# Softmax steps over the whole batch in even pairs, and a prologue in another order, in a fused softmax convolution and cosine feed-forward kernel

## The chip, the cores and the metric

The kernel runs on one core of one Trainium2 chip. Five engines run side by side, each through its own instructions in the order in which they were written: TensorE (PE, with its weight loads PEld), VectorE (DVE), ScalarE (ACT), GpSimd (POOL) and SyncE (SP), which issues the DMAs. The metric is device microseconds (us) of one execution.

## The reference

```python
w = weight_gen - np.max(weight_gen, axis=-1, keepdims=True)   # (8, 4096, 8 heads, 7 taps)
w = np.exp(w)
w = w / (np.sum(w, axis=-1, keepdims=True) + 1e-09)
x_pad = np.concatenate([np.zeros((B, K - 1, D)), x], axis=1)  # x (8, 4096, 192)
out = np.einsum('bshk,bskhg->bshg', w, x_unf)                 # x_unf: the 7 rows that end at s
...
h = x @ w_in        # x is that out, 32768 x 192; w_in 192 x 2048
g = h * np.cos(h)
return g @ w_out    # 2048 x 192
```

A causal convolution of seven taps, whose weights are a softmax per token and head, feeds a feed-forward layer with the activation h cos h. Inputs and output are float32; the two weight matrices arrive as 64-bit words.

## The kernel before

**Tiles.** The 32768 tokens are laid out as 128 partitions of 256 rows. A *block* is four rows of every partition (512 tokens); there are 64. The 2048 hidden columns are eight *pairs* of 128-column chunks, so the main loop (L678) runs over 64 x 8 = 512 pairs `i`, and eight pairs behind it (`j = i - LAG`) runs the second product. Each product is kept near float32 by splitting operands into a rounded `hi` and a bfloat16 `lo` rest.

**One pair of the loop** is a chain over three engines. PE makes `h` (1024 columns, PSUM, three buffers) from the block's `x_hi`, `x_lo`, `x_b` (`ffn_in_first` L428, `ffn_in_second` L445). ACT rounds it (`turn`, L455), DVE takes the fraction (L459), ACT the sine with a shift, the cosine (L463), DVE the product (L466), ACT the `ghi` part (L473) and DVE the rest `glo` (L477), after which the buffer of `h` is free. Eight pairs later PE multiplies `ghi` and `glo` by `w_out` (`ffn_out`, L519). Every second `ffn_out` carries transposes of one row of a later block (L407). With `k` the place of an `ffn_out` in its four, `evacuate` gives ACT the copies of the transposed row when k is 1 (L535, L536) and of the whole accumulator `part` when k is 3 (L541), both in odd pairs; the pair behind it gets ACT's `x_hi` and POOL's `x_b` and `x_lo` of that row (`split`, L385 to L390).

**POOL** mixes the blocks: `attention` (L331) is seven products of rows and tap weights (L344) and six adds (L359) per block, two steps per pair (three in some early pairs), one block after another; a block's transposes on PE need its last add, and `until_mixed` puts what is missing of a block into the program before PE's first transpose of it, at the pair with `i % 8 == 6`.

**The softmax** of 16 rows (four blocks) is one generator, `softmax` (L263), of which one step runs in each pair, behind that pair's other work; a batch starts at pairs 9, 41, 73, ... Its steps: load, maximum on DVE (L276), subtraction and clamp on POOL (L278, L285), then `powers` (L196) for the exponential without ACT's exponential table, on two halves of 448 columns in turn: nearest multiple (ACT, L206), rest (POOL, L209, L211), two squares (ACT, L214), their product (POOL, L217 to L221), the power of two (ACT, L224), one more square (ACT, L228) and the product (POOL, L231). Then the sum of the taps (POOL, `add_taps`, L187, and L297), the reciprocal (DVE, L303) and the scaling (POOL, L309). Batches with `early` set, the first three, use ACT's exponential (L282) before the sine table is loaded.

**Before the loop** the first block is mixed by `mix_first` (L634): DVE makes seven products, and PE transposes and adds each in PSUM (L631). Weights are converted from 64-bit words by `two_parts` (L128): ACT makes the size (L139), DVE three steps on the bits (L141, L145, L149), ACT the `hi` (L152) and POOL the `lo` (L155); the finished word stands in a tile `t` of which there are three. The table `late` (L590) tells at which pair the later weights are converted. PE's first pairs wait for these.

The program is written in the order in which every engine runs it (L755 to L763 pin that order), so the code sets what stands ahead of what in each queue.

Of the kernel before, what the change touches and what calls it, by code (L numbers as in the profile page):

```python
# [50 lines left out]
def tile_softmax_conv_then_cos_ffn(  # L51
# [76 lines left out]
    def two_parts(raw, hi, lo, half=None):  # L128
# [23 lines left out]
        nc.scalar.copy(out=hi, in_=bits.bitcast(F32))  # L152
# [2 lines left out]
        nc.gpsimd.tensor_tensor(out=lo, in0=bits.bitcast(F32), in1=hi.bitcast(F32), op=ALU.subtract)  # L155
# [40 lines left out]
    def powers(t):  # L196

        (a1, b1), (a2, b2) = EXP_A
        n = t.shape[1]
# [8 lines left out]
        def rest(k):
            nc.gpsimd.tensor_scalar(  # L209
                out=side[k], in0=whole[k], scalar1=-LN_2, scalar2=1.0, op0=ALU.mult, op1=ALU.mult)  # L210
            nc.gpsimd.tensor_tensor(out=t[k], in0=side[k], in1=t[k], op=ALU.add)  # L211

        def square(k, to, a):
            nc.scalar.activation(out=to[k], in_=t[k], func=AF.Square, bias=a, scale=0.5)  # L214

        def quartic(k):
            nc.gpsimd.tensor_scalar(  # L217
                out=side[k], in0=side[k], scalar1=b1, scalar2=1.0, op0=ALU.add, op1=ALU.mult)
            nc.gpsimd.tensor_scalar(
                out=t[k], in0=t[k], scalar1=b2, scalar2=1.0, op0=ALU.add, op1=ALU.mult)  # L220
            nc.gpsimd.tensor_tensor(out=t[k], in0=t[k], in1=side[k], op=ALU.mult)  # L221

        def power(k):
            nc.scalar.activation(  # L224
                out=whole[k], in_=whole[k], func=AF.Relu, bias=ONE_BITS, scale=2.0 ** 23)
# [568 lines left out]
```

## Time and profile before

| | |
|---|---|
| three runs, median (lowest to highest) | 2228.36 us (2226.72 to 2228.66) |
| the profiled execution | 2226.02 us |
| its span, first to last instruction | 2224.2 us |
| PE busy | 2160.8 us, 97% of the span |
| POOL busy | 2015.8 us, 91% |
| DVE, ACT busy | 1900.0 us (85%), 1869.2 us (84%) |
| mean granted clock of TensorE | 0.989 of full speed |

"Busy" leaves out waits; matmuls overlap, so a busy PE is not a PE at its peak. In a timeline row stand the start and the length in us, the engine, the source line, the operation, the tile written and the tiles read, their shapes and the count; the bracket gives the idle time of the engine before it and what ended it. The chain of work that ended last runs for 55% of the span on PE and for 40% on POOL. The granted clock is full from 90 us on; before, it changes between half and full. In 40 equal slices PE is busy in 5 to 7 tenths of the first two, and in 9 or more of all the others but the last.

### The profile page before, as it was taken

The numbers are of one execution on the slowest core, as the hardware profiler recorded it, in microseconds if no ns is written. First come the engines' busy times: TensorE is split into PE (matmuls) and PEld (weight loads), VectorE is DVE, ScalarE is ACT, GpSimd is POOL, SyncE is SP. The second block draws the span as 40 slices with busy tenths as digits, with TensorE's granted clock in tenths as the row PEclk, the third lists the DMA queues.
The fourth block names the chain that finished last, engine by engine and source line by source line (L and its number), as shares of the span: only waits on it lengthen the run. The fifth ranks groups of instructions, "written<-read, shape, count | busy, mean of one in ns | idle before, by whom it ended". The sixth has DMA issues, their size and how long they took to land.

```text
span 2224.2 us, 62220 instructions
## 1 busy us (share of the span) xinstructions
PE 2160.8 (97%) x26552; PEld 1677.8 (75%) x26552; DVE 1900.0 (85%) x1638; ACT 1869.2 (84%) x2352; POOL 2015.8 (91%) x1778
## 2 busy tenths in 40 slices
PE   5699999999999999999999999999999999999998
PEld 3477777777777777777777777777777777777777
DVE  6888888888888888888888888888888888888886
ACT  4688888988888898888988888888888988888885
POOL 8999999999999999999999999999999999989830
PEclk7899999999999999999999999999999999999999
DMA  7221221221221221211211221211212112212100
GB/s 176 49 48 34 56 48 38 51 48 39 51 56 30 59 48 30 60 43 43 52 42 45 48 50 39 56 42 40 56 34 56 48 34 56 48 36 48 30 16 19
DMA packets 53285, 105.67 MB, mean 48 GB/s; under 512 B 5791, under 2 KB 42135, under 8 KB 53007
## 3 DMA queue, kind: packets, MB, share of 16 engines
q1 hardware_dynamic: 53006, 101.69, 19.2%
q8 instruction: 208, 3.41, 0.7%
q14 instruction: 71, 0.57, 0.1%
HBM read 76.50 MB, written 25.17 MB: 46 GB/s over the span
## 4 chain that ended last, share of the span: by engine, by line
PE 55%; POOL 40%; issue 2%; ACT 1%; DVE 1%; DMA 0%; POOLq 0%; SPq 0%; ACTq 0%; DVEq 0%
PE acc L519 27%; PE h L445 17%; POOL xa L359 14%; POOL pr L344 11%; PE h L428 9%; POOL x_lo L390 3%; POOL part L550 2%; POOL taps L211 1%; POOL taps L221 1%; POOL taps L231 1%; POOL x_b L387 1%; POOL xa L344 1%; POOL den L193 1%; PE acc L407 1%; POOL side L209 1%
## 5 line engine op out<-in xcount | busy, mean ns | idle before, releaser
L459 DVE TENSOR_TENSOR turn<-h,turn 128x1024 f32<-128x1024 f32 x512 | 625.7, 1222 | 275.8 <-ACT turn L455 275.2
L519 PE MATMUL acc<-wo,ghi 64*128 64x384 f32 x8096 | 805.9, 336 | 1.8 <-DVE t L149 1.5
L519 PEld LDWEIGHTS acc<-wo,ghi 64*128 64x128 f32 x8096 | 724.5, 184 | 55.2 <-ACT part L541 10.8
L463 ACT ACTIVATE turn<-turn 128x1024 f32<-128x1024 f32 x512 | 541.7, 1058 | 216.3 <-DVE turn L459 216.3
L359 POOL TENSOR_TENSOR xa<-xa,pr 128x768 f32<-128x768 f32 (+1 forms) x384 | 698.6, 1819 | 1.7
L466 DVE SCALAR_TENSOR_TENSOR h<-h,turn 128x1024 f32<-128x1024 f32 x512 | 630.8, 1232 | 2.5 <-ACT turn L463 2.5
L477 DVE TENSOR_TENSOR glo<-h,ghi 128x1024 bf16<-128x1024 f32 x512 | 621.3, 1214 | 1.1 <-ACT ghi L473 1.1
L455 ACT ACTIVATE turn<-h 128x1024 int32<-128x1024 f32 x512 | 523.6, 1023 | 84.9 <-PE h L445 76.2
L344 POOL TENSOR_TENSOR pr<-xt,taps 128x768 f32<-128x768 f32 (+1 forms) x384 | 588.2, 1532 | 5.2
L473 ACT CAST ghi<-h 128x1024 fp32r<-128x1024 f32 x512 | 516.6, 1009 | 2.9 <-DVE h L466 1.3
L519 PE MATMUL acc<-wo_b,glo 64*128 64x192 bf16 x8096 | 462.5, 243 | 0.1
L519 PEld LDWEIGHTS <-glo 64*128 64x128 bf16 (+1 forms) x8128 | 318.1, 94 | 85.8 <-issue 67.7
L428 PE MATMUL h<-x_hi,wa_hi 64*128 64x512 f32 x1024 | 300.8, 583 | 0.0
L445 PE MATMUL h<-x_hi,wa_hi 64*128 64x512 f32 x1024 | 299.9, 582 | 0.0
L428 PE MATMUL h<-x_lo,wa_hi 64*128 64x512 bf16 x1024 | 199.0, 384 | 31.6 <-DVE glo L477 23.5
L445 PE MATMUL h<-x_hi,wb_hi 64*128 64x512 f32 x1024 | 204.2, 395 | 0.0
L428 PE MATMUL h<-x_b,wa_lo 64*128 64x512 bf16 x1024 | 196.7, 380 | 3.5 <-POOL wa_lo L155 3.5
L445 PE MATMUL h<-x_lo,wa_hi 64*128 64x512 bf16 x1024 | 196.0, 379 | 0.8
L445 PE MATMUL h<-x_b,wa_lo 64*128 64x512 bf16 x1024 | 196.2, 379 | 0.0
L445 PE MATMUL h<-x_lo,wb_hi 64*128 64x512 bf16 x1024 | 195.8, 379 | 0.0
L445 PE MATMUL h<-x_b,wb_lo 64*128 64x512 bf16 x1024 | 195.8, 378 | 0.0
L387 POOL TENSOR_SCALAR x_b<-x_hi 128x256 bf16<-128x256 f32 (+1 forms) x247 | 103.6, 420 | 93.0 <-ACT x_hi L385 90.6
(87 smaller groups left out, 2000.3 us busy)
## 6 DMA issues: line engine op xcount, KB each, us to landing
xt<-in_x_dram SPq DMA_DIRECT2D x62, 960.0 KB, 7.0
out_dram<-part SPq DMA_DIRECT2D x256, 96.0 KB, 2.2
taps<-in_weight_gen_dram SPq DMA_DIRECT2D x15, 448.0 KB, 4.5
raw<-in_moe_w_out_dram SPq DMA_DIRECT2D x8, 384.0 KB, 12.2
raw<-in_moe_w_in_dram SPq DMA_DIRECT2D x10, 256.0 KB, 11.1
xt<-in_x_dram SPq DMA_DIRECT2D x1, 768.0 KB, 10.0
xt<-in_x_dram SPq DMA_DIRECT2D x1, 540.0 KB, 5.5
raw<-in_moe_w_in_dram SPq DMA_DIRECT2D x4, 128.0 KB, 9.8
```

Of the source, the lines that this page charges most:

```text
L344: eng.tensor_tensor(out=dst.rearrange("p r (h g) -> p r h g", h=H), in0=xt[:, k + ra:k + rb, :].rearrange("p r (h g) -> p r h g", h=H), in ...
L359: eng.tensor_tensor(out=acc if k < K else xa, in0=acc, in1=old[:, ra:rb], op=ALU.add)
L387: nc.gpsimd.tensor_scalar(out=near[:, :, cs], in0=hi[:, :, cs].bitcast(F32), scalar1=1.0, scalar2=1.0, op0=ALU.mult, op1=ALU.mult)
L428: nc.tensor.matmul(h[:, q, :], lhsT=w[rs, chunk(pair, q)], rhs=v[rs, q, :], start=(m == 0), stop=False, skip_group_check=True)
L445: nc.tensor.matmul(h[:, 1 - q, :], lhsT=w[rs, cs], rhs=v[rs, q ^ middle, :], start=False, stop=(m == len(prods) - 1), skip_group_check=True)
L455: nc.scalar.activation(out=t.bitcast(I32), in_=hs[i], func=AF.Identity, bias=0.25, scale=1.0)
L459: nc.vector.tensor_tensor(out=t, in0=hs[i], in1=t.bitcast(I32), op=ALU.subtract)
L463: nc.scalar.activation(out=t, in_=t, func=AF.Sin, bias=SIN_BIAS, scale=SIN_SCALE)
L466: nc.vector.scalar_tensor_tensor(out=hs[i], in0=hs[i], scalar=TWO_PI, in1=turns.pop(i), op0=ALU.mult, op1=ALU.mult)
L473: nc.scalar.copy(out=hi, in_=hs[i])
L477: nc.vector.tensor_tensor(out=lo, in0=hs.pop(i), in1=hi.bitcast(F32), op=ALU.subtract)
L519: nc.tensor.matmul(to, lhsT=g[rs, n, t * P:(t + 1) * P], rhs=w[rs, fc, :], start=(lo == 0 and c == 0 and (k == 0 or whole and k == 1)), st ...
```

## The change

1. **Softmax of the later batches.** `powers` works on all 896 columns at once, with its ACT steps in even pairs (5, 9, 11, 13 and 17 pairs behind the batch's start, so 14, 18, 20, 22 and 26 for the batch that starts at pair 9). The maximum and the reciprocal on DVE are cut into two halves in two pairs. The sums come one pair later, the scaling two.
2. **`mix_first`** makes one product alone and the other six in pairs that DVE adds before PE transposes, through a PSUM tile `own_acc`.
3. **Order before the loop.** The copies of the first block's `x_hi` and `x_b` stand in the middle of the conversions, and `x_b` is made on ACT instead of POOL. The second weight conversion `w_a1` comes ahead of block 1's mixing, and its load ahead of that of block 1's rows. The exponential of the third batch and the load of the sine table move from ahead of the loop into pair 1.
4. **Words in place.** `two_parts` writes the finished word over the raw one instead of into `t`.
5. **`late`**: the third `w_out` piece and the last `w_in` piece are loaded before the loop, and all conversions are done a pair earlier.

```diff
@@ two_parts
-        bits = work.tile([P, CW], I32, name="t1", bufs=3)
-        size, bits = (shaped(t[:, 0:n], 1)[..., 0] for t in (room.pop(0), bits))
+        size = shaped(room.pop(0)[:, 0:n], 1)[..., 0]
...
-            out=bits, in0=low, scalar=29, in1=size, op0=ALU.logical_shift_right, op1=ALU.bitwise_or)
-        yield
-        nc.scalar.copy(out=hi, in_=bits.bitcast(F32))
+            out=low, in0=low, scalar=29, in1=size, op0=ALU.logical_shift_right, op1=ALU.bitwise_or)
+        yield
+        nc.scalar.copy(out=hi, in_=low.bitcast(F32))
...
@@ powers
+        nc.scalar.activation(out=whole, in_=t, func=AF.Identity, scale=1.0 / LN_2)
+        yield
+        nc.gpsimd.tensor_scalar(
+            out=side, in0=whole, scalar1=-LN_2, scalar2=1.0, op0=ALU.mult, op1=ALU.mult)
+        nc.gpsimd.tensor_tensor(out=t, in0=side, in1=t, op=ALU.add)
+        yield
+        yield from wait(2)
+        nc.scalar.activation(out=side, in_=t, func=AF.Square, bias=a1, scale=0.5)
+        yield
+        yield from wait(1)
+        nc.scalar.activation(out=t, in_=t, func=AF.Square, bias=a2, scale=0.5)
+        yield
...
+        yield
+        nc.scalar.activation(out=whole, in_=whole, func=AF.Relu, bias=ONE_BITS, scale=2.0 ** 23)
+        nc.gpsimd.tensor_tensor(out=t, in0=t, in1=side, op=ALU.mult)
+        yield
+        yield from wait(3)
+        nc.scalar.activation(out=t, in_=t, func=AF.Square)
+        yield
+        nc.gpsimd.tensor_tensor(out=t, in0=t, in1=whole.bitcast(F32), op=ALU.mult)
         yield
@@ softmax
-        nc.vector.tensor_reduce(out=top, in_=t, axis=AX.X, op=ALU.max)
-        yield
+        cut = (slice(0, n),) if early else (slice(0, n // 2), slice(n // 2, n))
+        for c in cut:
+            nc.vector.tensor_reduce(out=top[:, c], in_=t[:, c], axis=AX.X, op=ALU.max)
+            if early or c.start == 0:
+                yield
...
-        nc.vector.reciprocal(out=den, in_=den)
-        yield
+        for c in cut:
+            nc.vector.reciprocal(out=den[:, c], in_=den[:, c])
+            yield
@@ late
-        (-1, 2, w_in_a, (1280, 1792)), (-1, 2, w_out_2, (1,)), (0, 3, w_out_2, (2,)),
-        (0, 3, w_out_2, (3,)), (0, 4, w_in_a, (1792, 2048)),
-        (1, 4, w_out_2, (4,)), (2, 5, w_out_2, (5,)), (3, 6, w_out_2, (6,)),
-        (4, 7, w_out_2, (7,)),
+        (-1, 2, w_in_a, (1280, 1792)), (-1, 2, w_out_2, (1,)), (-1, 3, w_out_2, (2,)),
+        (-1, 3, w_in_a, (1792, 2048)), (0, 4, w_out_2, (3,)), (0, 4, w_out_2, (4,)),
+        (1, 5, w_out_2, (5,)), (1, 6, w_out_2, (6,)), (2, 6, w_out_2, (7,)),
@@ mix_first
+        for n, ks in enumerate(((K - 1,), (0, 1), (2, 3), (4, 5))):
...
+            if len(ks) == 2:
+                product(ks[0], own_acc)
+            product(ks[-1], pr[:, 0:RV])
+            if len(ks) == 2:
+                nc.vector.tensor_tensor(out=pr[:, 0:RV], in0=own_acc, in1=pr[:, 0:RV], op=ALU.add)
+            add_transposed(tr, pr, range(RV), n == 0)
@@ ahead of the loop
     go_on(w_a0, 1)
+    x_hi, x_lo, x_b = parts_of(0)
+    nc.scalar.copy(out=x_hi, in_=tr0)
     go_on(w_b0, 3)
+    all_of(w_b0)
+    nc.scalar.copy(out=x_b, in_=x_hi.bitcast(F32))
     go_on(sm1, 2)
     go_on(w_a0, 3)
-    all_of(w_b0, w_a0)
-    first = split(0, tr0, slice(0, CT), nc.vector)
-    go_on(sm1, 2)
-    go_on(first, 1)
-    all_of(first)
+    all_of(w_a0)
+    nc.vector.tensor_tensor(out=x_lo, in0=tr0, in1=x_hi.bitcast(F32), op=ALU.subtract)
+    go_on(sm1, 3)
     all_of(sm1)
+    make_room()
+    go_on(w_a1, 1)
+    go_on(sm2, 2)
+    go_on(w_a1, 3)
+    all_of(w_a1)
     bg = attentions()
-    go_on(bg, 2)
...
-    nc.scalar.activation(out=early, in_=early, func=AF.Sin)
     go_on(bg, 4)
@@ the loop
+        if i == 1:
+            next(sm2)
+            nc.scalar.activation(out=early, in_=early, func=AF.Sin)
```

How the queues stand then, at three places. The first is POOL in a cycle of the loop, from the last product ahead of the sums (`side`, `den`: the sum of the taps) to the next block. Before:

```order
L344 TENSOR_TENSOR pr<-xt,taps 128x768
L359 TENSOR_TENSOR xa<-xa,pr 128x768
L550 TENSOR_TENSOR part<-part 128x2x192
L190 TENSOR_TENSOR side<-taps 128x128x3
L193 TENSOR_TENSOR den<-side 128x128
L193 TENSOR_TENSOR den<-den,side 128x128
L193 TENSOR_TENSOR den<-den,taps 128x128
L297 TENSOR_SCALAR den<-den 128x128
L359 TENSOR_TENSOR xa<-xa,pr 128x768
L387 TENSOR_SCALAR x_b<-x_hi 128x2x128
L390 TENSOR_TENSOR x_lo<-part,x_hi 128x2x128
```

And with the change (its lines are those of the changed kernel):

```order
L331 TENSOR_TENSOR xa<-xa,pr 128x768
L522 TENSOR_TENSOR part<-part 128x2x192
L228 TENSOR_TENSOR taps<-taps,whole 128x896
L331 TENSOR_TENSOR xa<-xa,pr 128x768
L359 TENSOR_SCALAR x_b<-x_hi 128x2x128
L362 TENSOR_TENSOR x_lo<-part,x_hi 128x2x128
L189 TENSOR_TENSOR side<-taps 128x128x3
L192 TENSOR_TENSOR den<-side 128x128
L192 TENSOR_TENSOR den<-den,side 128x128
L192 TENSOR_TENSOR den<-den,taps 128x128
L268 TENSOR_SCALAR den<-den 128x128
```

The block's last add `xa`, which PE's transposes need, stands ahead of the five sums instead of behind them; the last product of the exponential is one operation and comes just before it.

The second place is ACT in the pairs of the squares (`side`, `taps`) of the same cycle. Before:

```order
L214 ACTIVATE side<-taps 128x448
L455 ACTIVATE turn<-h 128x1024
L473 CAST ghi<-h 128x1024
L463 ACTIVATE turn<-turn 128x1024
L541 COPY part<-acc 128x1024
L214 ACTIVATE taps<-taps 128x448
L455 ACTIVATE turn<-h 128x1024
L473 CAST ghi<-h 128x1024
L463 ACTIVATE turn<-turn 128x1024
L385 CAST x_hi<-part 128x2x128
L214 ACTIVATE side<-taps 128x448
```

With the change:

```order
L212 ACTIVATE side<-taps 128x896
L427 ACTIVATE turn<-h 128x1024
L445 CAST ghi<-h 128x1024
L435 ACTIVATE turn<-turn 128x1024
L513 COPY part<-acc 128x1024
L427 ACTIVATE turn<-h 128x1024
L445 CAST ghi<-h 128x1024
L435 ACTIVATE turn<-turn 128x1024
L357 CAST x_hi<-part 128x2x128
L215 ACTIVATE taps<-taps 128x896
```

The pair with the copy of `part` has no softmax step any more, and the pairs around it have a whole one.

The third place is POOL ahead of the loop, from the first `wa_lo` (of `two_parts`; `xt`, `pr`, `xa` are block 1's mixing). Before:

```order
L155 TENSOR_TENSOR wa_lo<-t_215,wa_hi 128x256
L387 TENSOR_SCALAR x_b<-x_hi 128x1024
L309 TENSOR_TENSOR taps<-taps,den 128x448
L344 TENSOR_TENSOR xa<-xt,taps 128x768
L344 TENSOR_TENSOR pr<-xt,taps 128x768
L278 TENSOR_TENSOR taps<-taps,top 128x896
L155 TENSOR_TENSOR wa_lo<-t_247,wa_hi 128x512
L344 TENSOR_TENSOR pr<-xt,taps 128x768
```

With the change:

```order
L154 TENSOR_TENSOR wa_lo<-raw,wa_hi 128x256
L281 TENSOR_TENSOR taps<-taps,den 128x448
L249 TENSOR_TENSOR taps<-taps,top 128x896
L154 TENSOR_TENSOR wa_lo<-raw,wa_hi 128x512
L316 TENSOR_TENSOR xa<-xt,taps 128x768
L316 TENSOR_TENSOR pr<-xt,taps 128x768 x2
```

The cast `x_b` is gone from POOL, and the two first operations of block 1 stand behind the second `wa_lo` instead of ahead of it.

More of the change, by code (lines that the diff above doesn't have):

```diff
@@ L213, in square @@
[L213 to L225, printed above, removed]
@@ L227, in again, with wait @@
-        def again(k):
-            nc.scalar.activation(out=t[k], in_=t[k], func=AF.Square)
-        def product(k):
-            nc.gpsimd.tensor_tensor(out=t[k], in0=t[k], in1=whole[k].bitcast(F32), op=ALU.mult)
-        near(0)
+        whole, side = (v[:, 0:t.shape[1]] for v in (whole_, side_))
+        def wait(n):
+            return [None] * n
+        nc.scalar.activation(out=whole, in_=t, func=AF.Identity, scale=1.0 / LN_2)
         yield
-        near(1)
-        rest(0)
+        nc.gpsimd.tensor_scalar(
+            out=side, in0=whole, scalar1=-LN_2, scalar2=1.0, op0=ALU.mult, op1=ALU.mult)
@@ L237, in powers @@
+        nc.gpsimd.tensor_tensor(out=t, in0=side, in1=t, op=ALU.add)
         yield
-        rest(1)
+        yield from wait(2)
+        nc.scalar.activation(out=side, in_=t, func=AF.Square, bias=a1, scale=0.5)
         yield
+        yield from wait(1)
+        nc.scalar.activation(out=t, in_=t, func=AF.Square, bias=a2, scale=0.5)
         yield
-        square(0, side, a1)
+        nc.gpsimd.tensor_scalar(
+            out=side, in0=side, scalar1=b1, scalar2=1.0, op0=ALU.add, op1=ALU.mult)
+        nc.gpsimd.tensor_scalar(
+            out=t, in0=t, scalar1=b2, scalar2=1.0, op0=ALU.add, op1=ALU.mult)
@@ L636, in mix_first, with product @@
         tr = ps_h.tile([P, 2, CT], F32, name="h")
-        for k in range(K):
-            tag, bufs = ("turn", TMP) if k % 5 < 3 else ("part", 2)
-            pr = work.tile([P, R, D], F32, name="pr", tag=tag, bufs=bufs)
+        def product(k, dst):
             nc.vector.tensor_tensor(
-                out=pr[:, 0:RV].rearrange("p r (h g) -> p r h g", h=H),
+                out=dst.rearrange("p r (h g) -> p r h g", h=H),
                 in0=rows[0][:, k:k + RV, :].rearrange("p r (h g) -> p r h g", h=H),
                 in1=t[:, :, :, k:k + 1].broadcast_to([P, RV, H, G]), op=ALU.mult)
-            add_transposed(tr, pr, range(RV), k == 0)
+        for n, ks in enumerate(((K - 1,), (0, 1), (2, 3), (4, 5))):
+            tag, bufs = ("turn", TMP) if n < 3 else ("part", 2)
+            pr = work.tile([P, R, D], F32, name="pr", tag=tag, bufs=bufs)
+            if len(ks) == 2:
[4 more added lines that the diff above has]
+            add_transposed(tr, pr, range(RV), n == 0)
         return tr
```

40 lines of the change are left out of this document (6 added, 34 removed).

## The prediction

> **What bounds the kernel now.** I read the busy time by stretches first. The bounds of the stretches are the starts of the last up-projection matmul (L445, `wb_hi`) of pairs 8, 32, 64, 96, 128, 448 and 480, so each stretch but the first (24 pairs) holds 32 pairs and the same matmuls. A softmax batch starts every 32 pairs; I call 32 pairs a cycle and number its pairs from a multiple of 32, so that a batch starts at pair 9. The columns are the stretch, its length, then busy us (instructions) of PE, PEld, DVE, ACT and POOL, the granted clock, DMA share and GB/s.
>
> ```profile
> 90.89:195.86 104.97, 101.97 (x1250) 77.92 (x1248) 87.56 (x75) 87.15 (x107) 102.15 (x85) 1.00 0.23 53
> 195.86:331.25 135.39, 133.57 (x1668) 104.43 (x1666) 116.25 (x99) 116.06 (x147) 128.02 (x113) 1.00 0.19 46
> 465.32:599.48 134.16, 133.22 (x1668) 103.78 (x1666) 116.24 (x99) 116.09 (x147) 127.81 (x113) 1.00 0.20 46
> 1940.61:2072.87 132.26, 132.26 (x1666) 104.12 (x1664) 115.10 (x99) 113.56 (x147) 120.78 (x115) 1.00 0.19 44
> ```
>
> The last row is a cycle whose batch is only four token rows long. There PE has no gap: 132.26 us, 4.133 per pair, is PE's floor. A full batch makes a cycle 134.11 long ((1940.61 - 331.25) / 12), so each of twelve cycles loses 1.85 us, the one from 195.86 loses 3.13, and the 24 pairs from 90.89 lose 5.8 (104.97 - 24 x 4.133). In all that is 31 us that PE work doesn't need. The next views show who takes it: the timeline of the cycle from 465.32, all engines.
>
> ```profile
> 528.16 1.01 POOL L550 TENSOR_TENSOR part<-part 128x384 f32<-128x384 f32 x1 [0.33 <-ACT part L541]
> ```
> ```profile
> 584.24 0.93 POOL L190 TENSOR_TENSOR side<-taps 128x384 f32<-128x384 f32 x1
> ...
> 586.00 0.40 PE L445 MATMUL h<-x_hi,wb_hi 64*128 64x512 f32 x2
> ...
> 587.41 0.95 DVE L303 RECIPROCAL den<-den 128x128 f32<-128x128 f32 x1 [0.48 <-POOL den L297]
> 587.46 1.82 POOL L359 TENSOR_TENSOR xa<-xa,pr 128x768 f32<-128x768 f32 x1
> ...
> 589.34 0.28 PE L407 MATMUL acc<-ident,xa 64*128 64x64 f32 x2 [0.87 <-POOL xa L359]
> ...
> 591.21 0.40 PE L445 MATMUL h<-x_hi,wb_hi 64*128 64x512 f32 x2
> ```
>
> **POOL** last waited for another engine at 528.16 (pair 15) and then ran 61.1 us without a stop until the add that ends at 589.28. PE needs that block at pair 30 and waits 0.87; from 586.00 to 591.21 its pair takes 5.21 instead of 4.13, so POOL's lateness costs about 1.05 per cycle. Ahead of that add stand the five sums of the softmax (584.24 to 587.46, 3.2 us).
>
> **ACT** takes most of the rest. Its rows around pair 22, and PE's for the same pairs (a `turn<-h` row is ACT's first step on one pair; the PE row is the start of the last matmul that it needs):
>
> ```profile
> 549.03 1.00 ACT L455 ACTIVATE turn<-h 128x1024 int32<-128x1024 f32 x1
> ...
> 553.47 1.00 ACT L455 ACTIVATE turn<-h 128x1024 int32<-128x1024 f32 x1
> ...
> 557.50 1.00 ACT L455 ACTIVATE turn<-h 128x1024 int32<-128x1024 f32 x1
> ...
> 561.65 0.58 ACT L224 ACTIVATE whole<-whole 128x448 int32<-128x448 int32 x1
> 562.13 1.01 ACT L455 ACTIVATE turn<-h 128x1024 int32<-128x1024 f32 x1
> ```
> ```profile
> 548.17 0.40 PE L445 MATMUL h<-x_hi,wb_hi 64*128 64x512 f32 x2
> ...
> 556.44 0.40 PE L445 MATMUL h<-x_hi,wb_hi 64*128 64x512 f32 x2
> ...
> 560.58 0.40 PE L445 MATMUL h<-x_hi,wb_hi 64*128 64x512 f32 x2
> ...
> 565.13 0.40 PE L445 MATMUL h<-x_hi,wb_hi 64*128 64x512 f32 x2
> ```
>
> With half a softmax step an even pair occupies ACT 4.03 (553.47 to 557.50) and an odd one 4.63, since the odd one also evacuates `part`; PE's pair is 4.13. Lateness piles up. When the step on an even pair's `h` starts 0.66 after that `h` is ready (557.50 against 556.44 + 0.40), the buffer of `h` comes free too late and PE's pair 24 takes 4.55 (560.58 to 565.13): 0.42 lost. Two pairs before, 0.46 late (549.03 against 548.17 + 0.40), it costs nothing: 548.17 to 556.44 is 8.27, two pairs at the floor. **DVE** adds 0.18: the whole maximum (1.08) delays it once, and PE's pair there is 4.31.
>
> ```profile
> 507.51 1.08 DVE L276 TENSOR_REDUCE top<-taps 128x128 f32<-128x896 f32 x1
> ```
> ```profile
> 510.79 0.40 PE L445 MATMUL h<-x_hi,wb_hi 64*128 64x512 f32 x2
> 515.10 0.40 PE L445 MATMUL h<-x_hi,wb_hi 64*128 64x512 f32 x2
> ```
>
> So 1.85 is 1.05 of POOL, 0.18 of DVE and 0.62 of ACT, the remainder.
>
> **The change, part by part: the cycles.** Rows for the new sizes come from the early batches and from groups by form (count | busy us, mean ns).
>
> ```profile
> 15.40 0.61 DVE L276 TENSOR_REDUCE top<-taps 128x64 f32<-128x448 f32 x1
> ...
> 22.00 0.54 DVE L303 RECIPROCAL den<-den 128x64 f32<-128x64 f32 x1
> ```
> ```profile
> L359 POOL TENSOR_TENSOR xa<-xa,pr 128x768 f32<-128x768 f32 x287 | 527.0, 1836 | 1.0
> ...
> L390 POOL TENSOR_TENSOR x_lo<-part,x_hi 128x256 bf16<-128x256 f32 x96 | 71.1, 740 | 0.0
> ...
> L211 POOL TENSOR_TENSOR taps<-side,taps 128x448 f32<-128x448 f32 x23 | 26.4, 1147 | 1.9
> ...
> L209 POOL TENSOR_SCALAR side<-whole 128x448 f32<-128x448 int32 x23 | 13.0, 566 | 1.7
> L285 POOL TENSOR_SCALAR taps<-taps 128x896 f32<-128x896 f32 x11 | 10.3, 936 | 1.0
> ```
> ```profile
> 28.46 0.95 ACT L282 ACTIVATE taps<-taps 128x896 f32<-128x896 f32 x1 [3.22 <-POOL taps L278]
> ```
>
> POOL: three scalar operations go from 2 x 0.566 to 0.936, 0.6 saved. Three two-input ones have no row at 896; between 1147 ns at 448 and 1836 at 768 lies 2.15 ns an element, so 2.11 against 2 x 1.147, 0.6 saved. Together 1.2 a cycle (at the least 0, if the long ones cost what two halves do; at the most 2.2, from 1.77 for the other two-input steps at 896). The order counts for more: the five sums now stand behind the add that PE waits for, another 3.2. The block is ready 4.4 earlier; PE, rid of most of ACT's delay, asks some 0.3 earlier, so the wait of 0.87 turns into 3.2 of room. The whole 1.05 goes, even with nothing saved by the merging.
>
> What is late next is the sum `den`: it ends 1.82 (the add) and 1.1 (`x_lo`, 0.74, and the smaller `x_b`) later, less 1.2, so 1.7 later. DVE's reciprocal waits for it, and behind that stand DVE's own steps of the pair, for which ACT and PE wait. But the reciprocal moves from pair 29 to pair 30, 4.1 later, less 0.3; DVE waited 0.48 and now has 3.8 - 1.7 - 0.48 = 1.6 to spare. The last product moves to pair 32; the block that reads it isn't mixed until PE has transposed the last row of the block two ahead, at pair 37.
>
> ACT: five steps of 0.95 in even pairs instead of ten of 0.57. An odd pair falls from 4.63 to 4.15 (561.65 to 562.13 less), an even one rises from 4.03 to 4.41. After one step ACT is 0.3 late, which costs nothing; the squares at pairs 18 and 20 follow each other with no recovery and make 0.03 + 0.28 + 0.02 + 0.28 = 0.61, between the 0.46 that cost nothing and the 0.66 that cost 0.42. On the line between them that is 0.32, once per cycle, since pairs 21 and 22 recover. So 0.30 of 0.62 is saved (bounds: all, if 0.61 is still inside the buffer; none, if pair 24 pays too).
>
> DVE: it is busy 116.24 of 134.16 us, so idle 0.56 in a pair; each half (0.61, 0.54) fits, and the 0.18 goes (0 to 0.18).
>
> The Trainium skill, "VectorE: DVE Perf Modes", section "The TRN2 errata — SBUF-src ops pay a fixed extra latency per instruction", speaks against the two splits: the latency is paid once by a large tile and by every one of many small ones. The trace agrees that a half costs more than half (the four rows of maximum and reciprocal); the case in which it would decide is a rival below.
>
> Thirteen cycles: DVE 13 x 0.18 = 2.3, ACT 13 x 0.30 = 3.9, POOL 12 x 1.05 and 3.13 - 0.80 = 2.3 in the first: 14.9. Together **21.1**.
>
> **The first 32 pairs.** Rows on POOL, PE and ACT:
>
> ```profile
> 7.05 3.41 DVE L640 TENSOR_TENSOR pr<-xt,h 128x576 f32<-128x576 f32 x5 [1.03 <-DMA xt<-in_x_dram]
> ```
> ```profile
> 19.82 1.01 ACT L385 CAST x_hi<-h 128x1024 fp32r<-128x1024 f32 x1 [1.63 <-PE h L631]
> ...
> 34.85 1.06 ACT L463 ACTIVATE turn<-turn 128x1024 f32<-128x1024 f32 x1 [0.51 <-DVE turn L459]
> ```
> ```profile
> 28.39 1.26 POOL L155 TENSOR_TENSOR wa_lo<-t,wa_hi 128x512 bf16<-128x512 f32 x1
> ```
> ```profile
> 85.89 1.01 POOL L155 TENSOR_TENSOR wo<-t,wo 128x384 fp32r<-128x384 f32 x1 [3.07 <-ACT wo L152]
> ```
> ```profile
> 104.08 1.02 POOL L550 TENSOR_TENSOR part<-part 128x384 f32<-128x384 f32 x1 [0.57 <-ACT part L541]
> ```
> ```profile
> 111.23 3.74 POOL L359 TENSOR_TENSOR xa<-xa,pr 128x768 f32<-128x768 f32 x2
> ```
> ```profile
> 115.21 0.22 PE L407 MATMUL acc<-ident,xa 64*128 64x64 f32 x2
> ```
> ```profile
> 184.88 0.95 DVE L303 RECIPROCAL den<-den 128x128 f32<-128x128 f32 x1 [3.85 <-POOL den L297]
> ```
>
> Two chains run here. *The conversions* on ACT and DVE get earlier. DVE now runs seven products and three adds of 0.68 (3.41 / 5), 7.05 to 14.1 with gaps; PE adds 26 times instead of 44 and ends some 2.2 behind them, so the first `x_hi` starts near 16.4, not 19.82. From there I went along each queue in its new order with the durations of the same operations before: the first `wa_lo` near 20.9, the second `wa_hi` 26.0, its `wa_lo` 27.3, then on ACT the first pair's step, the third exponential (0.95), the table load, the next `wa_hi`, and the first cosine near 30.6, not 34.85. In place, a word no longer waits for a `t` that POOL holds (1.2 once), and the last weights are done a pair earlier: by pair 8 this chain is some 5.4 ahead. *POOL* isn't. It ends that `wa_lo` near 27.3 instead of 29.65, but two mixing operations (1.54 each) that stood before it now stand behind, so it is 0.7 late. It gets back the 3.07 and the 0.57 for which it waited on ACT, so it is 2.9 ahead at 114.97, the end of the add for which PE (115.21) had 0.2 of room. PE is held there: **2.7** of the 5.4, with 0.2 for the stop (bounds: 5.4, and -0.7 if POOL's two waits stay).
>
> At pair 29 DVE waited 3.85 for `den` and PE lost about 3.4 (the 5.8 less 1.8 around the second block's transposes and 0.6 of ACT). Now `den` is 2.9 + 1.2 - 1.1 = 3.0 earlier, and the reciprocal 4.1 later less the 3.0 that PE has gained, 1.1: 3.85 - 3.0 - 1.1 is below zero, just. **3.4** (bounds: 0 and 3.4), and 0.3 of ACT.
>
> **The sum.** 21.1 + 2.7 + 3.4 + 0.3 = 27.5. The profiled execution took 2226.0 (span 2224.2 and 1.8 around it), so 2198.5 for it; the median of the runs is 2228.4, 2.4 higher, so **2200.9**. The last 250 us (from 1973) do not change.
>
> **Rivals.** *More*: ACT's 0.61 stays inside the buffer of `h` and PE gets the whole 5.4: 13 x 0.32 + 2.7 = 6.9 more, 2194. For it: 0.46 cost nothing; against it: POOL is busy 102 of the 105 us from 90.89. 0.14. *The wait moves to the reciprocal*: POOL delivers the block, but `den` ends later than worked out and DVE's stall costs PE 1.05 each cycle again; 13 x 1.05 = 13.7 lost, 2215. For it: DVE already waits for `den` in the cycle shown; against it: 1.6 of room. 0.12. *The halves cost*: DVE sets the pace, its 2 x 0.61 - 1.08 + 2 x 0.54 - 0.95 = 0.27 more a cycle are lost 14 times (3.8) and 2.3 isn't gained, 2207; against it, DVE's 0.56 of idle time per pair. 0.04. *Slower*: the long POOL operations stretch its 61 us until `den` stalls DVE in each cycle as at pair 29 now, 3.4 x 13 = 44 on top of the forecast, 2245. It decides once the stall costs PE 27.5 / 13 = 2.1 a cycle, for which `den` must come about 4.5 later than worked out. For it: POOL has no idle time in that stretch; against it: the rows at 896 are shorter than two halves. 0.07. *It doesn't do what it says*: POOL is late for a reason that the merging and the order leave alone, ACT's steps cost what they did, and what the start gains stays within 4 us: 0.05.
>
> **How the numbers follow.** The forecast keeps 0.58; its own range is 2194 to 2208 (ACT's bounds 0 and 8.1 against 3.9, the start's 5.4 and -0.7 against 2.7). With the two next cases the range is **2192 to 2215**. 0.2%, 4.5 us, is about what a measurement tells from no change: faster 0.58 + 0.14 + 0.12 + 0.04 = 0.88, same 0.05, slower 0.07.
>
> **What would show it.** In the profile after: cycles near 132.6; no wait of PE for POOL at the row transposes; no wait of the reciprocal for `den`; PE's pair 22 some 0.3 long and no other; the first cosine near 30.6; PE's first row transpose of block 3 still right behind POOL's add, near 112.3. The forecast is wrong if the cycles stay above 133.5, or if that transpose comes after 115.

## The result, and the profile after

| | before | changed |
|---|---|---|
| median (lowest to highest) | 2227.86 us (2226.72 to 2228.66) | 2208.01 us (2207.90 to 2208.20) |
| the profiled execution | 2226.02 us | 2208.10 us |
| its span | 2224.2 us | 2206.2 us |

The ratio is 0.9911, 95% interval 0.9899 to 0.9924: 19.9 us less. The forecast was 2200.9. The direction and the wide range held; the size was 27.5, and 19.9 came (18.0 between the two spans). The median before is here of four runs, one more than in the table ahead of the prediction.

The busy time by stretches, cut at the same pairs as in the prediction (8, 32, 64, 96, 128, 448, 480), with the same columns:

```profile
89.92:192.54 102.62, 101.67 (x1250) 78.24 (x1247) 89.11 (x77) 87.14 (x102) 100.87 (x79) 1.00 0.22 53
192.54:325.61 133.07, 133.07 (x1668) 105.65 (x1666) 116.58 (x101) 115.53 (x141) 127.97 (x108) 1.00 0.20 47
458.67:591.75 133.08, 133.07 (x1667) 103.76 (x1664) 116.60 (x101) 115.53 (x142) 126.78 (x107) 1.00 0.20 46
1922.35:2054.62 132.27, 132.27 (x1668) 104.12 (x1666) 115.32 (x101) 113.38 (x142) 119.15 (x108) 1.00 0.19 44
```

A full cycle now takes 133.08 instead of 134.16, so it still loses 0.81 against the 132.27 of the cycle with the tiny batch. The forecast had 132.6. Note the trap in these rows: PE reads as busy for 133.07 of 133.08, since the ends of matmuls are modelled and a wait of a quarter of a us disappears in them. The loss is seen only in the distance of PE's rows, or on its weight loads. The first stretch is 2.35 shorter (104.97 before). Set against the same pairs of before, the changed kernel is 0.97 ahead at pair 8, level at pair 16 (125.7 in both), and 3.32 ahead at pair 32.

**POOL is off the path.** The shares by engine of the chain that ended last (55% PE and 40% POOL before):

```profile
PE 94%; POOL 4%; DVE 1%; issue 1%; DMA 0%; ACT 0%; SPq 0%; POOLq 0%; DVEq 0%; ACTq 0%
```

The timeline around pair 30 of the same cycle, on POOL, PE and DVE:

```profile
576.18 1.84 POOL L331 TENSOR_TENSOR xa<-xa,pr 128x768 f32<-128x768 f32 x1
...
579.04 0.92 POOL L189 TENSOR_TENSOR side<-taps 128x384 f32<-128x384 f32 x1
...
581.93 0.30 POOL L268 TENSOR_SCALAR den<-den 128x128 f32<-128x128 f32 x1
```
```profile
581.67 0.22 PE L379 MATMUL acc<-ident,xa 64*128 64x64 f32 x2
```
```profile
584.34 0.54 DVE L275 RECIPROCAL den<-den 128x64 f32<-128x64 f32 x1
```

The block is ready at 578.02 and PE takes it at 581.67: 3.65 of room (3.2 forecast) where PE waited 0.87. The sum `den` ends at 582.23, the reciprocal starts 2.1 later (1.6 forecast) and waits for nothing.

**What is left is ACT, through the accumulator.** For two pairs of the cycle: ACT's step of the softmax (first row) and its copies of the accumulator to `part`; PE's last matmul of the up-projection in these pairs and the next; and the weight load with which PE starts the next accumulation, with the idle time of that queue ahead of it.

```profile
516.42 0.95 ACT L205 ACTIVATE whole<-taps 128x896 int32<-128x896 f32 x1
...
520.54 1.00 ACT L513 COPY part<-acc 128x1024 f32<-128x1024 f32 x1
...
554.18 1.00 ACT L513 COPY part<-acc 128x1024 f32<-128x1024 f32 x1
```
```profile
520.67 0.40 PE L417 MATMUL h<-x_hi,wb_hi 64*128 64x512 f32 x2
524.92 0.40 PE L417 MATMUL h<-x_hi,wb_hi 64*128 64x512 f32 x2
...
554.05 0.40 PE L417 MATMUL h<-x_hi,wb_hi 64*128 64x512 f32 x2
558.56 0.40 PE L417 MATMUL h<-x_hi,wb_hi 64*128 64x512 f32 x2
```
```profile
521.59 1.35 PEld L491 LDWEIGHTS acc<-wo,ghi 64*128 64x128 f32 x16 [0.26 <-ACT part L513]
...
555.23 1.35 PEld L491 LDWEIGHTS acc<-wo,ghi 64*128 64x128 f32 x16 [0.35 <-ACT part L513]
```

There is one accumulator. PE's next use of it starts at 521.59 and 555.23, each 0.05 behind the end of ACT's copy (521.54, 555.18). PE's pairs there take 4.25 and 4.51 instead of 4.13. Four of the five whole steps stand right ahead of a pair with such a copy; the fifth, at pair 20, stands ahead of one in which ACT copies and zeroes a row's part of the accumulator. In the changed kernel's cycle, three steps cost 0.11 each (the pairs that end at 16, 20 and 28 are that much longer), the two squares together 0.07 and 0.37 (22 and 24): 0.77, with some rows of 0.01 the 0.81. The same row stands in the profile of before, at the place where the prediction had blamed the buffer of `h`:

```profile
561.80 1.35 PEld L519 LDWEIGHTS acc<-wo,ghi 64*128 64x128 f32 x16 [0.34 <-ACT part L541]
```

That it was not the buffer of `h` can be read there too:

```profile
552.30 0.40 PE L445 MATMUL h<-x_hi,wb_hi 64*128 64x512 f32 x2
...
569.27 0.40 PE L445 MATMUL h<-x_hi,wb_hi 64*128 64x512 f32 x2
```
```profile
566.18 1.00 ACT L455 ACTIVATE turn<-h 128x1024 int32<-128x1024 f32 x1
```
```profile
511.76 1.36 PEld L519 LDWEIGHTS acc<-wo,ghi 64*128 64x128 f32 x16 [0.31 <-ACT part L541]
```

Before, ACT's step on `h` starts 0.77 late at pair 21 (the prediction's row at 553.47 against 552.30 + 0.40) and 0.65 late at pair 24 (566.18 against 565.13 + 0.40). PE's pairs there take 4.14 (552.30 to 556.44, 565.13 to 569.27), so this lateness of `h` cost nothing, though at pair 21 it was more than the 0.66 that the prediction blamed; no weight load waits for ACT in these two pairs. The last row belongs to the pair that DVE's whole maximum made 0.18 too long: that loss too came through the copy of the accumulator.

**The start** on DVE, ACT, POOL and PE:

```profile
9.06 0.75 DVE L611 TENSOR_TENSOR pr<-xt,h 128x576 f32<-128x576 f32 x1 [3.06 <-DMA xt<-in_x_dram]
9.90 0.76 DVE L611 TENSOR_TENSOR h<-xt,h 128x576 f32<-128x576 f32 x1
10.70 0.75 DVE L611 TENSOR_TENSOR pr<-xt,h 128x576 f32<-128x576 f32 x1
```
```profile
19.14 1.01 ACT L636 CAST x_hi<-h 128x1024 fp32r<-128x1024 f32 x1 [6.25 <-PE h L603]
...
33.14 1.05 ACT L435 ACTIVATE turn<-turn 128x1024 f32<-128x1024 f32 x1
...
49.15 1.01 ACT L445 CAST ghi<-h 128x1024 fp32r<-128x1024 f32 x1 [5.74 <-POOL wb_lo L154]
```
```profile
28.84 1.29 POOL L154 TENSOR_TENSOR wa_lo<-raw,wa_hi 128x512 bf16<-128x512 f32 x1 [0.94 <-ACT wa_hi L151]
```
```profile
115.16 0.28 PE L379 MATMUL acc<-ident,xa 64*128 64x64 f32 x2 [0.85 <-POOL xa L331]
```

DVE's first product waits for the rows until 9.06 (7.05 before), and the ten operations follow each other every 0.79 or so instead of every 0.68. So `x_hi` starts at 19.14 and not at 16.4, the second `wa_lo` ends at 30.13 and not at 27.3, and POOL, which then doesn't stop until it has finished block 3, lets PE go on at 115.16: 2.8 later than the forecast's 112.3, and where it was before. The conversions are late as well: the first cosine comes at 33.14 (34.85 before, 30.6 forecast). ACT's `ghi` then waits 5.74 for POOL's `wb_lo`, which before it did not, and PE is 0.97 ahead at pair 8 where the forecast had this chain 5.4 ahead.

### The profile page after: what moved, and what is told of

It reads as the page before. It is cut to its first block, busy times and chain, and to the rows that moved or that the text cites. A ratio compares the mean times of both kernels' runs of the same rounds, so it can differ in the third digit from the quotient of the medians.

```text
span 2206.2 us, 62053 instructions
## 1 busy us (share of the span) xinstructions
PE 2151.6 (98%) x26516; PEld 1676.4 (76%) x26516; DVE 1907.6 (86%) x1671; ACT 1862.9 (84%) x2278; POOL 2000.7 (91%) x1687
## 4 chain that ended last, share of the span: by engine, by line
PE 94%; POOL 4%; DVE 1%; issue 1%; DMA 0%; ACT 0%; SPq 0%; POOLq 0%; DVEq 0%; ACTq 0%
PE acc L491 47%; PE h L417 30%; PE h L400 15%; POOL xa L331 1%; PE acc L379 1%; POOL pr L316 1%; PE h L491 0%; POOL wo L154 0%; DMA xt<-in_x_dram 0%; POOL xa L316 0%; POOL wa_lo L154 0%; POOL taps L249 0%; DVE pr L611 0%; POOL taps L281 0%; DVE glo L449 0%
## 5 line engine op out<-in xcount | busy, mean ns | idle before, releaser
L491 PEld LDWEIGHTS acc<-wo,ghi 64*128 64x128 f32 x8096 | 724.9, 184 | 54.6 <-ACT part L513 16.4
```

What stands on the lines that cost most here:

```text
L491: nc.tensor.matmul(to, lhsT=g[rs, n, t * P:(t + 1) * P], rhs=w[rs, fc, :], start=(lo == 0 and c == 0 and (k == 0 or whole and k == 1)), st ...
```

## The experiments

They ran in three groups (the first four, the next four, the last four), each beside the kernel before; the record gives chip 1 for the first group and chip 14 for the other two. Medians compare within a group; across groups the ratio does. The changed kernel's own ratio is 0.9911.

| run | median, us | before in that group | ratio, 95% interval |
|---|---|---|---|
| softmax alone | 2208.27 | 2225.95 | 0.9921 (0.9908 to 0.9935) |
| start alone | 2225.42 | 2225.95 | 0.9999 (0.9990 to 1.0007) |
| taps in order | 2205.29 | 2225.95 | 0.9909 (0.9895 to 0.9922) |
| steps ahead of the cosine | 2197.36 | 2225.95 | 0.9873 (0.9860 to 0.9887) |
| halved powers | 2207.86 | 2227.76 | 0.9912 (0.9899 to 0.9926) |
| sums ahead of the add | 2207.84 | 2227.76 | 0.9912 (0.9898 to 0.9925) |
| whole maximum and reciprocal | 2209.91 | 2227.76 | 0.9922 (0.9908 to 0.9935) |
| both improvements | 2195.86 | 2227.76 | 0.9858 (0.9845 to 0.9872) |
| the change again | 2207.21 | 2225.82 | 0.9917 (0.9902 to 0.9931) |
| words in `t` | 2206.84 | 2225.82 | 0.9915 (0.9898 to 0.9931) |
| `x_b` on POOL | 2208.40 | 2225.82 | 0.9922 (0.9907 to 0.9937) |
| old mixing of the first block | 2208.97 | 2225.82 | 0.9925 (0.9910 to 0.9939) |

**The two halves of the change.** First the kernel before with only the new `powers` and `softmax`, then the changed kernel with only these two functions as before.

> The kernel before with the new softmax alone (whole powers in even pairs, halved maximum and reciprocal, sums one pair and scaling two pairs later); everything ahead of the loop, the conversions and the table of late weights stay as they were. Theory: the whole gain is the softmax's, because the start of the changed kernel is level with that of the kernel before at pair 14 (PE's first row transpose of block 3 at 115.16 there, 115.21 before), where PE waits for POOL. So PE starts as before (pair 8 at 90.9), that transpose comes near 115.2, the wait of 3.85 for the sum at pair 29 is gone, cycles take 133.08, and the time is 2208 to 2210. Rival: the new start is worth the 2.7 us of the forecast and the cycles less; then this kernel takes 2211 or more.

> The changed kernel with the softmax of the later batches as before (powers in halves, whole maximum and reciprocal, old pairs of the sums). Theory: the new start alone is worth nothing, 2227 to 2228.5: the first row transpose of block 3 comes near 115.2, the reciprocal at pair 29 still waits for the sum (3 to 4 us), cycles take 134.11. Rival: 2.7 us for the start, 2225.

Measured: 2208.27 and 2225.42. The second is by number the rival's 2225, but the kernel before takes 2225.95 in this group, so the gains are as the theory had them: 17.7 from the softmax, 0.5 from the start, which is inside what can't be told from nothing (ratio 0.9999). The cycles are 132.99 and 134.14. Of the start, PE's first row transpose of block 3 comes at 116.05 with the old start in this group and at 114.79 with the new one, so the new start may be worth a us or so, no more. (17.7 and 0.5 are 1.7 short of the 19.9 of both together, which was measured in another group; the intervals of the ratios overlap, so the runs don't tell this rest from nothing.) DVE's reciprocal of the second batch, with the softmax as before and with the new one:

```profile
184.60 0.95 DVE L302 RECIPROCAL den<-den 128x128 f32<-128x128 f32 x1 [3.96 <-POOL den L296]
```
```profile
186.61 0.54 DVE L276 RECIPROCAL den<-den 128x64 f32<-128x64 f32 x1
```

The wait goes with the softmax's part alone; the earlier start is not needed for it.

**The order of the taps in the first block**, in the changed kernel:

```diff
-        for n, ks in enumerate(((K - 1,), (0, 1), (2, 3), (4, 5))):
+        for n, ks in enumerate(((0,), (1, 2), (3, 4), (5, 6))):
```

> The changed kernel with the first block's products in the order of the taps: tap 0 alone, then the pairs 1 and 2, 3 and 4, 5 and 6, where the change has tap 6 alone and then 0 and 1, 2 and 3, 4 and 5. Taps 0 to 3 read the rows that the first, small transfer brings (landed at 6.99 in the changed kernel); tap 6 reads those of the large one (landed at 8.96). Theory: DVE's first product starts at 7.1 instead of 9.06, everything up to POOL's last add of block 3 comes 2.0 earlier, PE's first row transpose of block 3 near 113.1 instead of 115.16, time 2206.0. Rival: something else sets the start (a weight's landing, a wait for PSUM) and POOL's chain doesn't move: 2208.0.

DVE's first product, ACT's `x_hi`, and PE's transpose:

```profile
7.10 0.75 DVE L611 TENSOR_TENSOR pr<-xt,h 128x576 f32<-128x576 f32 x1 [0.97 <-DMA xt<-in_x_dram]
```
```profile
17.12 1.01 ACT L636 CAST x_hi<-h 128x1024 fp32r<-128x1024 f32 x1 [4.74 <-PE h L603]
```
```profile
113.07 0.28 PE L379 MATMUL acc<-ident,xa 64*128 64x64 f32 x2 [1.15 <-POOL xa L331]
```

Everything is 2.0 earlier: 7.10, 17.12 for 19.14, 113.07 for 115.16 (115.05 for the kernel of the next experiment, which has the changed kernel's start and ran in the same group). The time is 2205.29 where 2206.0 was expected. So the rows' arrival did not change; the change put a product first that needs the large transfer. The row also shows who sets the start: PE waits 1.15 for POOL, and 2.0 gained at the head of POOL's work arrive whole at pair 14. By medians, 2205.29 is 3.0 below the kernel with the softmax alone; the changed kernel itself did not run in this group, and the ratio to before can't tell the two apart.

**ACT's steps ahead of the cosine.** In every pair ACT waits 0.39 for DVE's fraction between `ghi` and the cosine. Here the five whole steps go into this gap, in pairs in which ACT copies neither `part` nor the row:

```diff
-        nc.scalar.activation(out=whole, in_=t, func=AF.Identity, scale=1.0 / LN_2)
+        gap.append(lambda: nc.scalar.activation(out=whole, in_=t, func=AF.Identity, scale=1.0 / LN_2))
...
             act_hi(i - 2)
+        for step in gap:
+            step()
+        gap.clear()
```

(the other four steps alike; `powers` starts one pair earlier, and its product stays one pair further from the sums)

> The changed kernel with its five whole ACT steps of a batch put between a pair's ghi and its cosine, where ACT waits 0.39 us for DVE's fraction in every pair, in pairs in which ACT copies neither the accumulator nor zeroes it; sums, reciprocal and scaling stay in their pairs. Theory: the 0.80 us that a cycle still loses are PE's waits for the single accumulator, freed by ACT's copy, which is late because each step is added to a pair whose 0.39 of idle time lies elsewhere; in the gap a pair with a step takes ACT 4.05, less than PE's 4.13, and the copy is on time. Cycles fall from 133.08 to 132.3, 13 of them give 10.4: 2197.6. Rival: PE waits for the buffers of h, and a cosine that comes 0.55 later makes these later still: cycles stay at 133 or above, 2208 or more.

The row of a cycle by stretches, and ACT's rows from a pair's `turn` to the next:

```profile
457.27:589.53 132.26, 132.26 (x1666) 104.12 (x1664) 116.54 (x101) 115.49 (x142) 126.59 (x107) 1.00 0.19 47
```
```profile
511.44 1.03 ACT L428 ACTIVATE turn<-h 128x1024 int32<-128x1024 f32 x1
512.36 1.01 ACT L446 CAST ghi<-h 128x1024 fp32r<-128x1024 f32 x1
513.25 0.96 ACT L207 ACTIVATE whole<-taps 128x896 int32<-128x896 f32 x1
514.10 1.06 ACT L436 ACTIVATE turn<-turn 128x1024 f32<-128x1024 f32 x1
...
515.57 1.03 ACT L428 ACTIVATE turn<-h 128x1024 int32<-128x1024 f32 x1
```

ACT's work in the cycle is the same (115.49 against 115.53 busy); only the place of 4.75 us of it is another. The pair takes 4.13 from `turn` to `turn`, no wait of PE for ACT is left, and the cycle is at its floor: 132.26. 2197.36 was measured, 2197.6 expected. This shows that the loss of 0.81 was the steps' place. That it went through the accumulator is what the waits of the changed kernel and of before show; the experiment by itself can't tell which of ACT's late operations PE felt.

**The exponential in halves again**, in consecutive pairs as before, all else of the change kept (`powers` as before, with one more `yield` at its end).

> The changed kernel with the exponential's steps in halves of 448 columns in consecutive pairs as before (pairs 14 to 26, product in 25 and 26); the sums, the reciprocal and the scaling stay in the changed kernel's pairs. Theory: whole steps cost a cycle 0.80 where halves cost 0.62 (the lengthened pairs of the two profiles), so cycles fall from 133.08 to 132.9 and the time by 13 x 0.18 = 2.3 to 2205.7; POOL's block is still ready well ahead of PE (3.65 of room, 1.2 less without the merging). Rival, the forecast's reading: halves cost ACT more than whole steps, and without the merging POOL is late again: cycles of 133.4 or more, 2212.

```profile
460.22:593.12 132.90, 132.83 (x1668) 104.06 (x1665) 116.53 (x101) 116.06 (x147) 127.67 (x113) 1.00 0.19 47
```

The cycle is 132.90 as expected: halves cost PE 0.64 there and whole steps 0.81, though ACT does more work with them (116.06 against 115.53). POOL kept 2.3 of room at pair 30, so the order of the sums alone makes it punctual. But the time did not fall to 2205.7. What the cycles gained was lost in the first two batches, where POOL without the merging is late again: in the first, DVE waits once more for `den`, and PE for a POOL operation behind the sums.

```profile
185.82 0.55 DVE L307 RECIPROCAL den<-den 128x64 f32<-128x64 f32 x1 [1.00 <-POOL den L300]
```
```profile
190.03 0.39 PE L432 MATMUL h<-x_lo,wa_hi 64*128 64x512 bf16 x2 [1.62 <-POOL x_lo L394]
```

Between pairs 28 and 32 PE gained 1.6 here on the kernel before where the changed kernel gained 3.4, and the pair that ends at 64 takes 0.47 too long. So the expectation was right for the cycles and wrong for the time.

**The sums ahead of the block's last add**, as before, the merged steps kept:

```diff
         nc.gpsimd.tensor_tensor(out=t, in0=t, in1=whole.bitcast(F32), op=ALU.mult)
-        yield
...
         if not early:
             yield
+            yield
```

> The changed kernel with the five sums one pair earlier, right behind the exponential's last product and so ahead of the block's last add, as before; reciprocal and scaling stay where they are. It tells the two causes of POOL's 1.05 apart, the order and the merging. Theory: the sums (3.2 to 3.3) eat most of the 3.65 of room at the first row transpose of pair 30, 0.4 is left, and PE still waits for nothing: cycles 133.08, 2208.0. Rival: the order alone made POOL punctual; PE waits again and the cycles are 133.5 or longer, 2213 or more.

POOL's last step of the sums and the add behind it, and PE's transpose:

```profile
579.51 0.30 POOL L267 TENSOR_SCALAR den<-den 128x128 f32<-128x128 f32 x1
579.89 1.85 POOL L331 TENSOR_TENSOR xa<-xa,pr 128x768 f32<-128x768 f32 x1
```
```profile
582.04 0.23 PE L379 MATMUL acc<-ident,xa 64*128 64x64 f32 x2
```

The block is ready at 581.74, PE takes it at 582.04: 0.30 of room, no wait, 2207.84 with cycles of 133.03. Each of the two, the order and the merging, would have done in the cycles; together they leave 3.65.

**Maximum and reciprocal whole on DVE** (`cut` is one slice; a `yield` keeps the pairs).

> The changed kernel with maximum and reciprocal on DVE whole again, each in the first of its two pairs (the reciprocal still at pair 30). Theory: the whole maximum (1.08) costs PE 0.17 to 0.18 once a cycle as it did before, 13 x 0.18 = 2.3, so 2210.3; the whole reciprocal (0.95) might cost as much again, 2212.6. Rival: the halves' fixed cost (0.27 more a batch) eats what they save; 2208 or less.

```profile
458.95:592.16 133.21, 133.21 (x1667) 103.67 (x1665) 116.23 (x99) 115.48 (x142) 126.80 (x107) 1.00 0.19 47
```

2209.91, 2.1 above the kernel with the sums ahead of the add, which ran in the same group, with the pair of the maximum 0.17 longer; the whole reciprocal costs 0.02. So the halved maximum is worth 2 us over the program and the halved reciprocal nearly nothing.

**Both improvements in one kernel**: taps in order and steps ahead of the cosine.

> The changed kernel with both edits: products of the first block in the order of the taps, and the whole ACT steps ahead of the cosine. They act at different places, so the gains add: PE's first row transpose of block 3 near 113.1, cycles 132.27 (no lengthened pair), 2195.3. Rival: POOL, which had 3.1 of room in the cycles of the second edit alone, or the sums take back a part: 2197.

```profile
455.34:587.61 132.27, 132.27 (x1668) 107.96 (x1665) 116.58 (x101) 115.56 (x142) 126.83 (x107) 1.00 0.19 47
```

2195.86, ratio 0.9858 (0.9845 to 0.9872), and PE's transpose at 113.37. Its interval lies below that of the changed kernel (0.9899 to 0.9924), so it beats both kernels. The cycles have nothing more to give: from pair 32 on no pair is longer than PE's floor.

**Three parts of the start**, beside the changed kernel in the same group. In the first the words stand in `t` again (`two_parts` as before); in the second POOL casts the first `x_b`; in the third `mix_first` is that of before.

> The changed kernel itself, on the chip of the next three runs, so that parts of the start, each worth about a us, are compared on one chip. Expected 2208.0, PE's first row transpose of block 3 near 115.2.

> The changed kernel with the finished words in the tile t again (three of them) and not over the raw ones. In the changed kernel ACT's ghi of pair 1 waits 5.74 for POOL's wb_lo (until 49.12): raw words and ghi share the slots of one pool, and a word in place holds its slot until POOL has read it. Theory: this wait goes, PE is earlier from pair 3 on, but POOL, without a stop from 28.8 to 115, still ends block 3 at the same time: first row transpose near 115.2, 2208.0. Rival: the wait sets the start, and without it the time falls by several us: 2204.

> The changed kernel with the first block's x_b cast by POOL (1.04 us) instead of ACT, in the same place of the program. Theory: POOL's chain sets the start, so all of it counts: first row transpose of block 3 at 116.2, 2209.0. Rival: POOL's idle time of 1.53 and 0.94 before block 1 swallows it: 2208.0.

> The changed kernel with the first block mixed as before (seven products in the order of the taps, each transposed and added by PE, no adds on DVE). Theory: DVE starts at 7.1, but PE's adds end the block near where they did before, so ACT's first x_hi starts near 19.8 where the changed kernel has 19.14; POOL's chain is 0.7 later, first row transpose of block 3 near 115.9, 2208.7. Rival: the pairs of products gained the forecast's 3.4 at x_hi, and without them the time rises by as much: 2211.

PE's first row transpose of block 3 in the changed kernel, with `x_b` on POOL, and with the old mixing:

```profile
114.65 0.28 PE L379 MATMUL acc<-ident,xa 64*128 64x64 f32 x2 [0.92 <-POOL xa L331]
```
```profile
115.82 0.28 PE L379 MATMUL acc<-ident,xa 64*128 64x64 f32 x2 [1.04 <-POOL xa L331]
```
```profile
116.31 0.28 PE L379 MATMUL acc<-ident,xa 64*128 64x64 f32 x2 [1.22 <-POOL xa L331]
```

Putting `x_b` on POOL costs 1.17 at that place and 1.19 in the time (2208.40 against 2207.21), as the theory of POOL's chain says. The old mixing costs 1.66 there and 1.76 in the time, not 0.7: DVE starts at 6.79, but then waits twice for PE's adds, and `x_hi` comes at 20.39 where the changed kernel has 18.69 in this group.

```profile
10.56 0.75 DVE L611 TENSOR_TENSOR pr<-xt,h 128x576 f32<-128x576 f32 x1 [0.36 <-PE h L602]
13.12 0.76 DVE L611 TENSOR_TENSOR pr<-xt,h 128x576 f32<-128x576 f32 x1 [1.81 <-PE h L602]
```

With the words in `t` the wait of 5.74 is gone:

```profile
43.03 1.00 ACT L446 CAST ghi<-h 128x1024 fp32r<-128x1024 f32 x1
```

and the time does not move (2206.84 against 2207.21, less than the spread between runs). Raw words and `ghi` share one pool of slots; in place, a word keeps its slot until POOL has read it. But the theory's reason is not what the trace shows. PE is not earlier from pair 3 on: its last up-projection matmul of pairs 3, 4 and 8 starts at 45.69, 55.37 and 90.68, and in the changed kernel of this group at 45.52, 54.66 and 89.33. Another wait for the same operation of POOL has taken the place of the one of `ghi`. DVE has to write its next word to a `t` that POOL's `wb_lo` is still reading, here (first row) and in the kernel before (second row):

```profile
48.85 0.56 DVE L149 SCALAR_TENSOR_TENSOR t<-raw,acc 128x384 int32<-128x384 int32 x1 [3.15 <-POOL wb_lo L155]
```
```profile
48.99 0.56 DVE L149 SCALAR_TENSOR_TENSOR t<-raw,acc 128x384 int32<-128x384 int32 x1 [1.23 <-POOL wb_lo L155]
```

So the run does not show that a wait of 5.74 is free; it shows that POOL's `wb_lo` holds the conversions at 49 us in all three kernels. In this profile PE also has no wait for POOL at pair 14: the block is ready at 114.62, and PE takes it at 114.92.

## Why the prediction was right in sign and too large

Each term of its sum, with what the traces show:

| term | predicted | measured |
|---|---|---|
| POOL in the cycles | 14.9 | 14.9 (1.05 in 12 cycles, 2.3 in the first) |
| DVE | 2.3 | 2.3 (13 x 0.18; 2.1 when undone) |
| ACT in the cycles | 3.9 | -2.4 (0.62 became about 0.80: 13 x -0.18) |
| start | 2.7 | 0.0 |
| wait for `den` at pair 29 | 3.4 | 3.4 |
| ACT in the first batch | 0.3 | -0.1 |
| sum | 27.5 | 18.1 (18.0 between the spans) |

**What held.** POOL's lateness was read rightly: the whole 1.05 goes, even with nothing saved by the merging, which the halved powers show (2.3 of room). The price of the merged operations held (2.10 to 2.12 for 2.11 worked out, 0.94 for 0.936). `den` didn't become the next wait, and the wait at pair 29 went, though not "just": it needs none of the gain of the start. The Trainium skill, "VectorE: DVE Perf Modes", section "The TRN2 errata — SBUF-src ops pay a fixed extra latency per instruction", had spoken against the splits. DVE's busy time in the cycle is indeed 0.36 larger with them (116.60 against 116.24), as the fixed cost of a tile says, but undoing them costs 2.1: idle time of DVE paid for it.

**The step on ACT failed**, and of all terms it was furthest off. It said that after one step ACT is 0.3 late, "which costs nothing", because before a lateness of 0.46 had cost nothing and one of 0.66 had cost 0.42 through "the buffer of `h`". The two rows were compared without asking what ACT does next. The 0.46 came ahead of a pair in which ACT does not copy the whole accumulator, the 0.66 ahead of one in which it does; the 0.77 and the 0.65 that cost nothing were not read. PE waits for the copy, and that leaves about 0.25 of room, counted as the lateness of the step on `h` in the pair of the copy: 0.36 late cost 0.11, 0.62 late cost 0.37. The change put every whole step ahead of a copy or a zeroing of the accumulator, so each one costs something, where the halves cost in two pairs of the cycle. For the two squares, 0.61 of lateness and a loss of 0.32 were worked out; 0.62 and 0.37 came, plus 0.07 two pairs earlier. The three steps that were to be free cost the rest. Making ten steps into five saved ACT work, and PE lost more.

**The start failed at its first number.** The forecast let DVE begin at 7.05 as before and gave an operation 0.68. But the product that the change puts first reads the rows of the large transfer, which lands 2.0 later, and the ten operations came every 0.79. That is the 2.8 by which `wa_lo` and PE's transpose were late, so nothing of 2.7 was left. The order of the products stood in the diff; what was not asked is which of the two transfers each product needs. Why an operation takes 0.79 there was not separated: five products that only write their own tile follow each other every 0.68 (the row at 7.05, and again with the old mixing), those that go through the PSUM tile and are added do not. That POOL holds PE at pair 14 was right for the changed kernel (0.85), and it is why 2.0, 1.2 and 1.7 us at the head of POOL's queue arrived nearly whole there, and the 1.2 and 1.7 in the time. The margin is small: in four of the runs (softmax alone, steps ahead of the cosine, sums ahead of the add, words in `t`) PE comes 0.2 to 0.4 behind POOL and waits for nothing there.

The other chain of the start failed too. The forecast had the conversions 5.4 ahead by pair 8; PE was 0.97 ahead there. Part of it is the late `x_hi`: the first cosine came 2.5 behind the forecast. The rest is that this chain is not free of POOL. The forecast saw only that words in place free `t` and so took away a wait of 1.2; a new wait of `ghi` for the same `wb_lo` came in its place. `wb_lo` ends at 49.12, and before at 48.96, so there the lead was gone, and the 0.97 was won behind it. As the changed kernel ran, about one us was there to keep, not 2.7, even if POOL had been on time at pair 14.

**The median.** The 2.4 by which before's median lay above its profiled execution were added to the forecast. The changed kernel's median equals its profiled one (2208.0 and 2208.1), and in the three groups of experiments before's own median was 2225.8 to 2227.8. So the forecast of the profiled execution, 2198.5, was 9.6 too low, and 7.1 in the median. None of the rivals happened: the cycles are 133.08, below the 133.5 that were named as the sign, but the transpose comes after 115, which was the other sign and did tell.

## What to carry to other kernels

A lateness has no price of its own: ask which buffer the late engine's next operations free, and how soon after that operation another engine needs it. Work that doesn't fit into a full engine's pair can be free in the gap where that engine waits for an answer inside its own chain: moving five steps of 0.95 us in each cycle ahead of the dependent one, without saving any of them, was worth about 10 us here. When products are put into another order, look up which transfer each of them reads.

## What the runs showed that was not expected

- PE's waits of 0.1 to 0.4 us don't show in its busy time: 133.07 of 133.08 in a cycle that loses 0.81. They show on the weight loads, whose queue had 0.26 and 0.35 of idle time ahead of the load that ACT's copy released.
- A wait of 5.74 us on ACT, made by the change and taken away again, did not move the time by more than 0.4: with it gone, DVE waited for the same operation of POOL through another buffer. A wait that an edit removes can come back under another name, so look where the next engine starts, not only whether the wait is gone.
- Between the three groups the kernel before had medians of 2225.8 to 2227.8, the lowest and the highest of them on a chip of the same number, while the changed kernel's were 2207.2 and 2208.0. Differences of a us at the start are readable only against a run in the same group or at a place in the trace.
